# A dilated convolution in one list: more six-step groups, and every instruction placed one by one

## The chip, the cores and the metric

The kernel runs on one core of a Trainium2 chip. The metric is the device time of one execution in microseconds; the median of three runs of the kernel before is 263.8 us (262.93 to 263.85).

## The reference

The input `x` has 2 sequences of 16,000 time steps with 256 channels; `w` holds three taps of 256 by 512, `w_o` is 256 by 256, everything in bf16. It is a causal convolution of three taps with dilation 2, a gate, and a projection:

```
xp = jnp.pad(x, ((0, 0), (4, 0), (0, 0)))
h = sum over i of einsum('btc,cd->btd', xp[:, 4 - 2*i : 4 - 2*i + T, :], w[i])
z = tanh(h[..., :256]) * sigmoid(h[..., 256:])
return z @ w_o
```

## The kernel before

Time is cut into groups. A group of R rows (256, if nothing else is said) holds J steps per row, so it covers J times R time steps; its tile `xt` has channels on the partitions and one plane of R columns for each step. One group P (four steps, 160 rows) is computed directly. All others save multiplications: an output group is made from a few products of sums and differences of `xt`'s planes with sums of the weights, and is then put together by adding and subtracting the products.

- Kind B covers 4 steps with 4 products per block: operands `m`, `p`, `d0`, `d3`.
- Kind A covers 6 steps with 5 products: operands `u1`, `rm`, `rp`, `r0`, `ri`. The last four are each a sum of two tiles: `rp` is `f` plus `u1`, `rm` is `e` plus `u3`, `r0` is `u0` plus `uh`, `ri` is `u2` plus `ud`, where `u3`, `uh`, `ud` are `u1` times a constant. The second term is added onto the first, in place.

Each group has four blocks, one for each 128 of the 512 output channels. For a block the steps are, by the letters of the plan: F, M, L, Z (first, mid, last, zero) accumulate their products in PSUM bank `b`, I (inf) in bank `a`. Between them other engines read the bank: ScalarE copies it after F into `ss` (c, line 432); VectorE makes `hh` from `ss` and `b` (h), writes `a` from `ss` and `b` (a, on line 435 like the others), and for kind A `yy` from `hh` and `b` (y). Then ScalarE applies tanh or sigmoid to `b`, `a` and `yy` (line 475), VectorE multiplies the two (g, the gate, line 494), TensorE multiplies by `w_o` (P, line 512), and ScalarE or VectorE (v) converts the result (e, lines 537 and 521) for a store issued by SyncE.

Before, 13 groups are of kind A and 12 of kind B (10 of 256 rows, one of 160, one of 128), beside P. Four B groups come first, then A and B blocks alternate in proportion. The operands come from three places. VectorE makes most of them whole (128x1024, lines 380 and 382). GpSimd makes `ri` and many of B's in quarters (128x256, line 382), each held behind a VectorE instruction by a semaphore, so that it runs while VectorE works on PSUM. And the second terms of `rm`, `rp` and `r0` are added by an accumulating DMA from SBUF to SBUF, issued from GpSimd's queue (line 377):

```
        if name in BY_DMA:
            return nc.gpsimd.dma_start(out=G[name][:, :, :, :R], in_=b, accum_op=op)
```

The loads of `xt` are transposing DMAs on SyncE's queue (line 234), which also issues the stores. The order is written out by hand: `PLAN` has a line for each block's turn, with one column of letters for each engine. Loads are issued up to 15 turns ahead (`LOAD`).

Of the kernel before, what the change touches and what calls it, by code (L numbers as in the profile page):

```python
# [11 lines left out]

PLAN = """
 |  | m.0 d3.0 p.0 d0.0 G | 
F D D | c w |  | 
F L D | c d | a d3.1 G | wa.4 wa.3
F L Z I P P | c b e | a | wa.6
Z L F I | a b c | m.1 d0.1 p.1 a | wa.12'
F L Z I | a c b | m.2 g a | wa.5
L P F Z I | a e c b | d3.2 a | wa.2'  # L20
Z L F I | a b c | d0.2 u0.0 g a | wa.7
F L Z I | a c b | f.0 u1.0 a | wa.1
L F Z I | a c b | p.2 a u2.0 g | wa.14'
L Z F I P | a b e c | e.0 d3.3 a | wa.0
F P P Z L I | a c e e b | p.3 ud.0 g a | wa.11
L F I Z P P | a c b | u1.1 m.3 m.4 a | rp.0 ri.0'
F L Z P I P | a e e e b c | u3.0 e.1 uh.0 a d0.3 f.2 g | wa.10
F I Z L P | a c e b | u1.2 a | rm.0 ri.0'
L F Z I | a e c b | a g | r0.0
L Z I F P | a b c | u3.1 p.4 a | wa.8  # L30
Z L F P I | a b c e e | u0.1 uh.2 f.1 a d0.4 g | ri.0'
F I L P Z M P | c e a b | d3.4 u2.1 ud.1 a h | rp.1 rm.1 wa.15' wa.13' wa.9'
F Z L M I | a c e e b | g uh.1 a y h | d3.5' d3.5' ri.0'
P P Z F L I | y a b c | u3.2 e.2 a y | r0.1 ri.1 m.5
F L I Z M | a c y b | a u0.2 h | d0.5 d0.5
Z F L I M | a b c e | g a y h | r0.2 d0.5 ri.1
F P Z I L | a e c b y | g u2.2 a y | rm.2 ri.1 m.5' d0.5
F L P I Z M | a e c y b | a e.3 h | p.5
Z F I L M | a c b | g a y h | p.5 p.5 ri.1
P P F Z L I | a e e y c b | u0.3 a y | m.5 m.5'  # L40
L F I Z M | a c y b | ud.2 a u1.3 h | ri.2 ri.2'
Z P P F L I P M | a b e c e e | g u3.3 a y h | rp.2 p.5' p.6' d0.6'
F Z I L P | a e b c y | f.3 g a y | ri.2 d3.5
F L I Z M | a c y b | a u2.3 h | d3.5
Z F I L M P P | a c b e | g a y h | rp.3 rm.3 d0.6 ri.2
F Z I L P | a e e y b c | uh.3 e.4 ud.3 a y | d3.6 p.6 ri.3''
F L I Z M | a c y b | a u1.4 h | ri.3
Z F I L M P P P | a c b e | g a y h | m.6 d3.6
F Z P L I | a e y c b e e e | g u0.4 u3.4 f.4 a y | r0.3 ri.3 m.6''
F L P I Z M | a c y b | a ud.4 h | d0.6 d3.6 m.6  # L50
Z I F L | a b c | g a y | ri.3 m.6
F L P I Z M P | c a y b | u2.4 a h | ri.4' d3.6
F Z L I P M | a e e c b | e.5 uh.4 y a h | rp.4 p.6
F Z P L I | a y c b e e | g f.5 a y | rm.4 p.6' d0.6'
F P L Z M I | a c y b | g a h | r0.4 p.7 p.7 ri.4 d3.7 d3.7 m.7
F Z L P M I | a c e b e | u1.5 a y h | ri.4
I Z P L F P P | a e e b c y | u0.5 a y | ri.4
F L Z I M | a c b y | ud.5 u1.6 u2.5 a h u3.5 g | rp.5 ri.5''
F P Z L I P M | a c e e b | a y h | rm.5 d0.7 p.7
F Z I L P | a e y b c e | g uh.5 a y | m.7' ri.5  # L60
F L I Z P M | a c y b | g ud.6 a h | r0.5 ri.5' m.7'
F P Z L M I | a c b e e | e.6 uh.6 y a h | d3.7 d0.7
F P Z L I P | y e a b c | f.6 a y | m.7' ri.5
F L Z M I P | a c y b e | u0.6 g h u3.6 a | rp.6 p.7' d0.7' d0.7
F L P M Z I | a c e e e b | y a h | rm.6
Z I L F P | a y b c | u2.6 u1.7 a y g | m.8' m.8'
F P P L Z M I | a c e y b e e | g u3.7 a h | r0.6 ri.6' d3.7'
F Z L P I M | a c b | e.7 ud.7 a y h | p.8' ri.6' ri.6
F Z I L P P | a y b c | u0.7 u2.7 a y | p.8' ri.6'
F L P M Z I | a e c y e e b | uh.7 f.7 a h g | d0.8' ri.7'  # L70
Z I F L | a b c | u1.8 a y | rm.7 rp.7 m.8'
F P P L Z M I | a c e y b e | g a e.8 h | d3.8 ri.7
F Z I L M P | a c b e | g a y ud.8 h | p.8 d3.8 ri.7
F P Z I L P | a e c y b e | u3.8 f.8 a y | r0.7 d3.8' d0.8
L F I Z M P | a e c b y | a u0.8 h | d0.8 m.8
F Z P L P M I P | a c e e e b | e.9 g a y h | p.8 ri.7
Z F L I | a b c y | u1.9 g a y | rp.8 d3.8
F L I Z M P P | a c e b y | u2.8 ud.9 a h | rm.8 d0.8 d3.9'
Z F L P M P I P | a e c e e b | uh.8 g a y h | ri.8 ri.8
Z L F I | y a b e c | u3.9 u2.9 a y | r0.8 ri.8  # L80
F I Z L M P P | a c y b | f.9 u0.9 a h | ri.9' ri.8'
F L Z I M | a e e c b | g y a h | ri.9
F Z I L | y a b c e | f.10 g a y | rp.9 d0.9
F P P L Z M I | c a b y | u0.10 a h | rm.9 d0.9'
F Z I L P P M | a e c e b | e.10 g uh.9 y a h | r0.9 d3.9
F P Z L P I | a e e y b c e | m.9 u1.10 a y | ri.9' ri.9
F L I Z M P | c a e b y | p.9 a h | d0.9' d3.9' d3.9'
Z P F L I M | a b c e e | ud.10 g a y h | d0.9
F I Z P L P | a y b c | u2.10 g a y | rp.10 ri.10 d3.10 d0.10
F L I Z M | a c e y b | a u1.11 h |   # L90
Z P F L P I | a b c e | u3.10 g y uh.10 a | rm.10 ri.10'
F L P Z I M | a e c b e y | e.11 a u2.11 h | ri.10'
F I Z L P P M | c a e b | ud.11 f.11 a y u3.11 h | r0.10 ri.10'
F I Z L | a e c y b e | g uh.11 a y | d3.10 d0.10'
L P F P Z M I | a c b y | g a h | rm.11 d0.10 d3.10
F Z L I M P | a c e b | u1.12 a y h | ri.11' ri.11'
F Z I L | a e c b y | p.10 m.10 y a | rp.11 ri.11
L P F P Z M I | a c e b y e | a u3.12 u0.11 h f.12 g | d3.10
Z F P L I P M P | a c b e | a y h | r0.11 ri.11 d0.10
I F Z L P | a e y e b e c | g e.12 ud.12 y a | rm.12  # L100
F P P M Z L P I | c e a b y e | p.11 u2.12 uh.12 a h g | d3.11' ri.12'
F I L P Z M P | a c e b | y a h | d0.11 d3.11
F Z L P I | y e a b c e e | u0.12 m.11 a y | rp.12 r0.12 ri.12''
F P Z L M I | c a b y | a h g | 
F Z L P I M P | a c b e e e | a y h | d0.11 ri.12
F Z L P I | a c b e y | g a y | d3.11 ri.12
L F I Z M P | a c y b e e | a g h | 
Z F L P I P M | b c a | y a h | 
F P Z L I | a e e y b c e | y a | d0.11
F P L Z M I | c a b y | a h g | d0.11  # L110
F P L Z I P | a e c b e | a y | d3.11
F I Z L | a c y b | g a | 
L P I F Z P | a e b c e | a g | 
Z I F L P P | a c b E | a v | 
L Z I P p | a b | a g v | 
Z I P p P | a e b | v | 
H H | a e E | g v | 
R R |  |  | 
 | e | v | 
"""  # L120


@with_exitstack
def kernel(
    ctx: ExitStack,
    tc: tile.TileContext,
    x: bass.AP,
    w: bass.AP,
    w_o: bass.AP,
    out: bass.AP,  # L130
):
# [33 lines left out]
    for b in range(B):  # L165
        t = 0
        if b == 0:
            t = group("P", b, 0, 160)
# [374 lines left out]

# [182 lines left out]
```

## Time and profile before

| what | value |
|---|---|
| median of three runs | 263.8 us |
| profiled execution, span from first to last instruction | 261.4 us |
| taken as the profiled execution's own time (the span and 2.4 us around it, to the median) | 263.8 us |
| TensorE busy | 256.5 us, 98% |
| ScalarE busy | 243.7 us, 93% |
| VectorE busy | 240.5 us, 92% |
| GpSimd busy | 136.2 us, 52% |
| matmuls | 1484 |

A page of the profile gives the busy time of each engine (PE is TensorE, DVE is VectorE, ACT is ScalarE, POOL is GpSimd, SP is SyncE), the busy share in 40 slices, the DMA queues, the chain of work that ended last and the costliest groups of instructions. In a group's row stand the line, the engine, the operation, the tile written and those read, the shape, the count, then the busy time in us and the mean duration of one in ns, then the idle time before them. A duration includes an overlap with the next instruction, so that counts times means add up to more than the engine's busy time.

### The profile page before, as it was taken

To read this page: it belongs to the slowest core of one execution; us is meant where nothing else is said; L and a number is where in the kernel's file an instruction comes from. 1 tells how busy PE (TensorE), PEld (TensorE's weight loads), DVE (VectorE), ACT (ScalarE), POOL (GpSimd) and SP (SyncE) were. 2 spreads that over 40 slices of the span, in tenths; PEclk is the share of its full clock that TensorE was granted. 3 is DMA by queue.
4 is the path that set the end of the run, shared out by engine and by line. 5 is a ranking of instruction groups with operands and counts; after the bars stand their busy time and mean duration, and the time that the engine had idled before them with its cause. 6 is when DMAs were issued, how large, how long until landed. Compare 5 with 4: busy or idle time off the path is not lost.

```text
span 261.4 us, 4534 instructions
## 1 busy us (share of the span) xinstructions
PE 256.5 (98%) x1484; PEld 144.2 (55%) x1484; DVE 240.5 (92%) x401; ACT 243.7 (93%) x492; POOL 136.2 (52%) x204
## 2 busy tenths in 40 slices
PE   8999999999999999999999999999999999999993
PEld 5654565545545555555555555555555555665682
DVE  2899999999999999999999999999999999977773
ACT  4989998999999999999999999999999999999993
POOL 1033355687765577956757685643746453431100
PEclk9999999999999999999999999999999999999999
DMA  6999979999969667969895799959825574462115
GB/s 185 215 168 212 262 177 174 227 211 179 212 152 232 139 147 143 228 147 230 197 197 135 175 214 190 239 160 201 237 41 127 149 152 116 129 160 109 76 61 210
DMA packets 81663, 45.20 MB, mean 173 GB/s; under 512 B 68936, under 2 KB 70216, under 8 KB 81640
## 3 DMA queue, kind: packets, MB, share of 16 engines
q1 hardware_dynamic: 75112, 33.74, 54.6%
q0 software_dynamic: 5616, 10.23, 23.2%
q10 hardware_dynamic: 912, 0.95, 1.1%
q8 instruction: 11, 0.18, 0.3%
q14 instruction: 12, 0.10, 0.1%
HBM read 1.25 MB, written 16.38 MB: 67 GB/s over the span
## 4 chain that ended last, share of the span: by engine, by line
PE 97%; DMA 1%; DVE 0%; issue 0%
PE b L401 57%; PE o_ps L512 21%; PE a L401 16%; PE b L421 1%; PE a L421 1%; DMA xn<-in_x_dram 1%; PE tp L308 0%; DVE osb L521 0%; PE fill L248 0%
## 5 line engine op out<-in xcount | busy, mean ns | idle before, releaser
L435 DVE SCALAR_TENSOR_TENSOR a<-ss,b 128x512 f32<-128x512 f32 (+2 forms) x100 | 67.1, 672 | 7.9 <-ACT sg L475 3.1
L537 ACT CAST osb<-o_ps 128x512 bf16<-128x512 f32 x119 | 69.8, 622 | 0.8 <-PE o_ps L512 0.7
L512 PE MATMUL o_ps<-wo_sb,zz 128*128 128x256 bf16 x496 | 70.5, 273 | 0.0
L432 ACT COPY ss<-b 128x512 f32<-128x512 f32 (+2 forms) x100 | 59.6, 597 | 4.6 <-PE b L401 3.5
L512 PEld LDWEIGHTS <-zz 128*128 128x128 bf16 x496 | 48.4, 98 | 25.2 <-DVE zz L494 0.2
L401 PEld LDWEIGHTS <-w_sb 128*128 128x128 bf16 x400 | 39.0, 98 | 36.8 <-issue 0.2
L382 POOL TENSOR_TENSOR u<-u,ud 128x256 bf16<-128x256 bf16 x52 | 39.8, 772 | 24.9 <-DVE zz L494 9.1
L382 POOL TENSOR_TENSOR d<-xt 128x256 bf16<-128x256 bf16 (+2 forms) x56 | 33.4, 606 | 32.7 <-DVE zz L494 13.0
L494 DVE TENSOR_TENSOR zz<-th,sg 128x1536 bf16<-128x1536 bf16 (+2 forms) x52 | 40.9, 788 | 0.5 <-ACT sg L475 0.2
L435 DVE SCALAR_TENSOR_TENSOR yy<-hh,b 128x512 f32<-128x512 f32 x52 | 35.4, 680 | 1.9 <-PE b L401 1.8
L435 DVE SCALAR_TENSOR_TENSOR hh<-ss,b 128x512 f32<-128x512 f32 x52 | 35.4, 681 | 1.2 <-PE o_ps L512 0.5
L475 ACT ACTIVATE sg<-b 128x512 bf16<-128x512 f32 (+2 forms) x50 | 30.5, 610 | 2.1 <-PE b L401 1.4
L475 ACT ACTIVATE th<-b 128x512 bf16<-128x512 f32 (+2 forms) x50 | 30.5, 610 | 1.9 <-PE b L401 1.6
L475 ACT ACTIVATE sg<-a 128x512 bf16<-128x512 f32 (+2 forms) x50 | 31.0, 619 | 0.0
L401 PE MATMUL b<-f,wp_sb 128*128 128x512 bf16 x104 | 30.9, 379 | 0.0
L401 PE MATMUL b<-u,w_sb 128*128 128x512 bf16 x104 | 30.9, 379 | 0.0
L401 PE MATMUL a<-u,w_sb 128*128 128x512 bf16 x104 | 30.9, 379 | 0.0
L401 PE MATMUL b<-u,wa_sb 128*128 128x512 bf16 x104 | 30.9, 379 | 0.0
L401 PE MATMUL b<-e,wm_sb 128*128 128x512 bf16 x104 | 30.9, 378 | 0.0
L475 ACT ACTIVATE th<-a 128x512 bf16<-128x512 f32 (+2 forms) x50 | 30.5, 614 | 0.3 <-PE a L401 0.2
L401 PEld LDWEIGHTS <-wp_sb 128*128 128x128 bf16 x200 | 19.5, 98 | 20.1 <-issue 0.7
L401 PEld LDWEIGHTS <-wm_sb 128*128 128x128 bf16 x200 | 19.5, 98 | 17.0 <-issue 0.4
(59 smaller groups left out, 342.7 us busy)
## 6 DMA issues: line engine op xcount, KB each, us to landing
out_dram<-osb SPq DMA_DIRECT2D x26, 384.0 KB, 2.6
out_dram<-osb SPq DMA_DIRECT2D x23, 256.0 KB, 3.0
f<-u POOLq DMA_DIRECT2D x13, 256.0 KB, 3.5
e<-u POOLq DMA_DIRECT2D x13, 256.0 KB, 4.4
u<-uh POOLq DMA_DIRECT2D x13, 256.0 KB, 5.3
w_sb<-in_w_dram ACTq DMA_DIRECT2D x3, 256.0 KB, 4.1
xt<-in_x_dram SPq DMA_TRANSPOSE x25, 7.2
xn<-in_x_dram SPq DMA_DIRECT2D x1, 160.0 KB, 3.2
```

Of the source, the lines that this page charges most:

```text
L382: ins = eng.tensor_tensor(out=o, in0=a, in1=b, op=op)
L401: nc.tensor.matmul(G[bank, oi][:, :2 * R], lhsT=wmat[:, ct, osl], rhs=G[mv][:, :, ct, :R], start=which == "first" and ct == 0, stop=ct == ...
L421: nc.tensor.matmul(G[bank, oi][:, :4 * r].rearrange("p (j r) -> p j r", j=4), lhsT=w_taps[tap][:, ct, osl], rhs=xt[:, j0:j0 + 4, ct, c0 + ...
L432: nc.scalar.copy(out=G["ss", oi][:, :n], in_=G["b", oi][:, :n])
L435: return note(nc.vector.scalar_tensor_tensor(out=out, in0=in0, scalar=scalar, in1=in1, op0=ALU.mult, op1=op))
L475: nc.scalar.activation(out=G[name, dt][:, j:j + 2, :R], in_=G[bank, oi][:, :2 * R].rearrange("p (q r) -> p q r", q=2), func=(ACT.Tanh, ACT ...
L494: note(nc.vector.tensor_tensor(out=G["z"][:, dt, :, :n], in0=G["th", dt][:, :, :n], in1=G["sg", dt][:, :, :n], op=ALU.mult))
L512: nc.tensor.matmul(o_ps[:, q, :], lhsT=z, rhs=wo_sb[:, dt, :], start=dt == 0 and (q == 0 or len(dts) == NT), stop=dt == NT - 1, skip_group ...
L537: copy(out=osb[:, 2 * jp:2 * jp + 2, :], in_=o_ps[:])
```

## The change

The groups are written down (`GROUPS`): P, 18 groups of kind A, three B groups of 256 rows and one of 160. `ORDER` runs their blocks group after group: the three B groups, then all A groups, then the last B. The plan with a line per turn is replaced by one list of 1,745 tokens in which every instruction has its place among all engines' instructions. Besides:

- `ri` gets its second term by accumulating DMA too. In all 69 such DMAs are listed (token `rp.3d`), where there were 39; two `rm` and one `ri` are left to VectorE (`rm.5`, `rm.9`, `ri.8`).
- Quarters of `u0`, `u1`, `u2`, `e`, `f` and of the last B groups' operands are given to GpSimd one by one (`u0.3q38`). The number behind q says how many VectorE instructions back the one lies that the quarter waits for.
- For 31 of the 72 A blocks `hh` is a plain copy of the bank made by ScalarE (k), and `yy` is then made from that copy and `a` instead of from `hh` and `b`.
- VectorE makes 25 of the output conversions (v), instead of 5.
- Loads (x) and stores (s) are tokens of the list; the rotating buffers of operands, `hh`, th, sg and output tiles are fixed slots numbered by group or block; the scratch tiles of the weights lie in the A groups' gate tiles.

The diff, cut to its core:

```
-PLAN = """
- |  | m.0 d3.0 p.0 d0.0 G | 
-F D D | c w |  | 
...
+GROUPS = (
+    "P160 A A A A A A A A B B B",
+    "A A A A A A A A A A B160",
+)
+ORDER = """
+9 9 9 9 10 10 10 10 11 11 11 11 1 1 1 1 2 2 2 2 ... 21 21 21 21 22 22 22 22
+"""
+PLAN = """
+m.0 d0.0 d3.0 p.0 D D m.1 D F G d F c G F c p.1 L d3.1q1 c P A w L d0.1 x e0 L d3.1q1 Z A I b f.0 P a u1.0 Z d3.1q1
+F A b I c u0.0 F a Z x d0.2 c I g wa.3q1 b L L a A d3.1q12 P e1 F A wa.5q12 Z c ud.0 I u1.1 b Z a x u3.0 L m.2 b F
...
+P y f.13q158 Z Y e75 M ri.12d e.13 b Z ri.13d e76 h48 I b F rm.13d u1.14 P a g f.13q1 L c F y Y I y A P rp.13d c M
...
-    wu_sb = [[ss_pool.tile([P, D2], f32, name=f"wu{tap}", tag=tag) for tag in ("hh", "yy")] for tap in range(K)]
+    wu_ct = [z_pool.tile([P, K, D2], f32, name="wu", tag="zz6") for _ in range(CT)]
+    wu_sb = [[wu_ct[ct][:, tap, :] for ct in range(CT)] for tap in range(K)]
...
-    BY_DMA = ("rm", "rp", "r0")
...
-                G[name] = pool.tile([P, 2, CT, RG], bf16, name=name, tag=name)
-        if name in BY_DMA:
+                G[name] = slot(name, G["n"], [P, 2, CT, RG])
+        if eng is None:
             return nc.gpsimd.dma_start(out=G[name][:, :, :, :R], in_=b, accum_op=op)
...
+    def second(blk, on_act):
...
+        if on_act:
+            G["k", oi] = True
+            nc.scalar.copy(out=G["hh", oi][:, :n], in_=G["b", oi][:, :n])
+            return
         stt(G["hh", oi][:, :n], G["ss", oi][:, :n], 1.5, G["b", oi][:, :n], ALU.subtract)
...
-            stt(G["y", oi][:, :n], G["hh", oi][:, :n], 2.0, b)
+            if ("k", oi) in G:
+                stt(G["y", oi][:, :n], G["hh", oi][:, :n], -2.0, G["a", oi][:, :n])
+            else:
+                stt(G["y", oi][:, :n], G["hh", oi][:, :n], 2.0, b)
...
+    def on_gpsimd(token):
+        token, _, back = token.partition("q")
+        behind = made_v[-1 - int(back)]
...
+        had = quarters.get((g, name), 0)
+        quarters[g, name] = had + 1
+        pre(g, name, nc.gpsimd, slice(had, had + 1), behind=behind)
...
+    for token in PLAN.split():
+        what = token[0]
+        if "." in token:
+            if "q" in token:
+                on_gpsimd(token)
+            elif token[-1] == "d":
+                pre(*group_of(token[:-1]), None)
             else:
-                made.append(todo.pop(0))
...
+                note(pre(*group_of(token), nc.vector))
+        elif what in "FMLZI":
+            product(next(kinds[what]), {"F": "first", "M": "mid", "L": "last", "Z": "zero", "I": "inf"}[what])
...
+        elif what == "s":
+            store(*stores[int(token[1:])])
+        elif what == "x":
+            load(next(to_load))
```

More of the change, by code (lines that the diff above doesn't have):

```diff
@@ L209, with slot @@
     ctx.enter_context(tc.manual_schedule())
+    SLOTS = {"m": 2, "p": 2, "d0": 3, "d3": 3, "u0": 3, "u1": 3, "u2": 3, "e": 3, "f": 3, "u3": 2, "uh": 2, "ud": 2, "hh": 3, "th": 2, "osb": 3, "odd": 3}
+    def slot(name, n, shape, dtype=bf16, kind=None):
+        return ring_pool.tile(shape, dtype, name=name, tag=f"{name}.{n % SLOTS[kind or name]}")
     def warm_up(n):
@@ L351, in operand @@
         }[name]()
+    blocks = [0] + [g for g, oi in seq if oi == 3]
+    a_seq = [blk for blk in seq if blk[0] in As]
     def hold(ins, behind):
@@ L441, in halfway @@
         n = 2 * G["R"]
[L442 removed]
+        G["hh", oi] = slot("hh", a_seq.index(blk), [P, 2 * RG], f32)
+        if on_act:
+            G["k", oi] = True
+            nc.scalar.copy(out=G["hh", oi][:, :n], in_=G["b", oi][:, :n])
+            return
         stt(G["hh", oi][:, :n], G["ss", oi][:, :n], 1.5, G["b", oi][:, :n], ALU.subtract)
@@ L465, in activate @@
         if (name, dt) not in G:
-            G[name, dt] = act_pool.tile([P, J, RG], bf16, name=name, tag=f"{name}{J}")
+            same = [at for at in blocks if groups[at]["J"] == J]
+            G[name, dt] = slot(f"{name}{J}", NT * same.index(g) + dt, [P, J, RG], kind="th")
         if G["kind"] == "P":
@@ L705 @@
+    assert next(todo, None) is None and next(to_load, None) is None
 _INS = ['x', 'w', 'w_o']
```

386 lines of the change are left out of this document (126 added, 260 removed).

## The prediction

> **What bounds the kernel now.** I read the page first: the span, TensorE's row, the engines' shares of the chain that ended last, and the two large DMA queues.
>
> ```profile
> span 261.4 us, 4534 instructions
> PE 256.5 (98%) x1484; PEld 144.2 (55%) x1484; DVE 240.5 (92%) x401; ACT 243.7 (93%) x492; POOL 136.2 (52%) x204
> ...
> q1 hardware_dynamic: 75112, 33.74, 54.6%
> q0 software_dynamic: 5616, 10.23, 23.2%
> ...
> PE 97%; DMA 1%; DVE 0%; issue 0%
> ```
>
> The chain is TensorE nearly from end to end. Whether the others have room is a question by stage, so next come the windows: for each stretch its length, each engine's busy time with its instructions, the granted clock and the DMA engines' share.
>
> ```profile
> 0.00:10.00 10.00, 9.16 (x65) 5.82 (x66) 5.10 (x8) 6.44 (x14) 0.81 (x8) 1.00 0.79 196
> 10.00:20.00 10.00, 10.00 (x59) 5.41 (x58) 8.90 (x18) 8.54 (x18) 2.55 (x5) 1.00 1.12 183
> ...
> 240.00:250.00 10.00, 10.00 (x68) 6.48 (x67) 7.25 (x13) 9.98 (x24) 1.20 (x3) 1.00 0.21 81
> 250.00:262.00 12.00, 7.30 (x67) 6.20 (x64) 6.17 (x12) 7.22 (x19) 0.00 (x0) 0.95 0.39 147
> ```
>
> ```profile
> 20.00:60.00 40.00, 40.00 (x217) 21.00 (x215) 39.55 (x68) 37.51 (x74) 22.08 (x32) 1.00 1.10 207
> 60.00:200.00 140.00, 140.00 (x784) 76.26 (x782) 136.80 (x223) 134.86 (x268) 92.17 (x130) 1.00 0.83 181
> ```
>
> Between 10 and 250 us TensorE never stops. VectorE is busy 98.9% of 20 to 60 us and TensorE still does not wait: nearly full engines can be fed here. The DMA share over 1 means that several queues' packets were in flight on one engine. So the time can fall only by less TensorE work, and it falls by that much only if the others keep up.
>
> **TensorE.** The chain in order of time gives the price of a piece (start, length, what):
>
> ```profile
> 58.93 1.29 PE b L401 x6
> ```
>
> A matmul of 512 columns takes 1.29/6 = 0.215 us, one of 256 I take at half, 0.108. Products of 512 columns go from 840 (13 A groups x 4 blocks x 10 matmuls, 10 B groups x 4 x 8) to 816 (18 x 40 + 3 x 32); the 32 of 256 columns go with the 128-row group; those of 160-row groups and the projection stay. Saved: 24 x 0.215 + 32 x 0.108 = 8.6 us, all on the path. If nothing else bound, the span would be 261.4 - 8.6 = 252.8 us.
>
> **VectorE and ScalarE.** Groups by form (busy us, mean ns of one, idle before):
>
> ```profile
> L435 DVE SCALAR_TENSOR_TENSOR a<-ss,b 128x512 f32<-128x512 f32 x92 | 63.4, 690 | 3.9 <-PE b L401 2.6 <-ACT th L475 0.6
> L432 ACT COPY ss<-b 128x512 f32<-128x512 f32 x92 | 55.9, 608 | 4.6 <-PE b L401 3.5 <-DVE u L382 0.3 <-ACT sg L475 0.3
> ...
> L475 ACT ACTIVATE sg<-b 128x512 bf16<-128x512 f32 x46 | 28.6, 621 | 1.9 <-PE b L401 1.4
> L382 DVE TENSOR_TENSOR u<-xt 128x1024 bf16<-128x1024 bf16 x39 | 27.9, 720 | 0.0
> ...
> L494 DVE TENSOR_TENSOR zz<-th,sg 128x1536 bf16<-128x1536 bf16 x26 | 24.8, 954 | 0.5 <-ACT sg L475 0.2
> ...
> L475 ACT ACTIVATE th<-yy 128x512 bf16<-128x512 f32 x26 | 17.2, 660 | 0.2 <-DVE yy L435 0.2
> L494 DVE TENSOR_TENSOR zz<-th,sg 128x1024 bf16<-128x1024 bf16 x20 | 13.7, 683 | 0.0
> ...
> L380 DVE TENSOR_SCALAR ud<-u 128x1024 bf16<-128x1024 bf16 x13 | 5.7, 441 | 0.0
> ...
> L521 DVE CAST osb<-o_ps 128x512 bf16<-128x512 f32 x5 | 3.3, 685 | 0.6 <-PE o_ps L512 0.6
> ```
>
> The smaller forms I price at half of these; other B operands and two gate forms are priced by the rows shown. VectorE, counted in the two instruction lists: whole sums 87 to 64, -23 x 0.72 = -16.6; four small ones gone, -1.4; scalings 39 to 54, +15 x 0.441 = +6.6; PSUM sums of 512 columns 196 to 197, +0.7, and four small ones gone, -1.4; gates of 1536 columns 26 to 36, +9.5, of 1024 20 to 6, -9.6, small ones -0.7; conversions 5 to 24 and a small one, +13.3. Sum +0.4 us: nothing. ScalarE: `ss` copies 92 to 84 and four small, -6.1; 31 bank copies k, +18.8; tanh and sigmoid of `b` and `a` -16 x 0.621 and eight small, -12.4; of `yy` 52 to 72, +13.2; conversions 119 to 100 and a small one, -12.1. Sum +1.4 us.
>
> So both keep their work in a shorter span. VectorE did 14.0 us of its 240.5 in the first 20 us, whose work is nearly the same; the other 226.5 in 252.8 - 20 is 97%, below the 98.9% shown above. ScalarE: 243.7 + 1.4 - 15.0 = 230.1 in 232.8, 99%; the row of 240 to 250 shows it at 9.98 of 10. At 252.8 us both are full but not over; about 2 us more make room. The new wait, I behind `yy` in the 31 k blocks (`yy` reads `a` before I adds to it), has in the list at least one other TensorE token between, and what queues behind it is TensorE itself: I take it at nothing while VectorE is on time, and at what VectorE is late otherwise.
>
> **GpSimd.**
>
> ```profile
> L382 POOL TENSOR_TENSOR u<-u,ud 128x256 bf16<-128x256 bf16 x52 | 39.8, 772 | 24.9 <-DVE zz L494 9.1 <-DVE yy L435 4.4 <-DVE u L382 3.5
> ...
> L377 POOL DMA_DIRECT2D f<-u x13 | 11.9, 918 | 0.0
> ```
>
> Quarters of 256 columns go from 124 to 164 (40 x 0.772 = 31 us), DMA issues from 39 to 69 (30 x 0.918 = 28). 136.2 + 59 = 195 us of some 257: 76%, not a bound over the whole.
>
> **The DMA engines** are where the work goes. The 39 accumulating DMAs took 23.2% of 261.4 us = 60.6 us of all 16 engines, 1.55 us each; 30 more cost 46.6 us. Loads and stores move nearly the same bytes. From 77.8% (203.4 us) the two queues come to 250 us in about 255: full. What this costs depends on when an accumulating DMA lands against when its product is due. Before, by windows (median us from issue to landing, last), first 20 to 60 us, then 60 to 200:
>
> ```profile
> e<-u POOLq DMA_DIRECT2D x3, 256.0 KB, 7.7
> u<-uh POOLq DMA_DIRECT2D x3, 256.0 KB, 8.3
> f<-u POOLq DMA_DIRECT2D x2, 256.0 KB, 5.6
> ```
>
> ```profile
> f<-u POOLq DMA_DIRECT2D x9, 256.0 KB, 3.4
> e<-u POOLq DMA_DIRECT2D x8, 256.0 KB, 4.3
> u<-uh POOLq DMA_DIRECT2D x7, 256.0 KB, 5.3
> ```
>
> Means of the three: 7.2 us at a DMA share of 1.10, 4.3 at 0.83. By the Trainium skill, "DMA: Bandwidth & Descriptors", section "Anatomy of one DMA", a DMA from GpSimd's queue takes about 2.0 us plus its bytes at 436 GB/s, an estimate of 2.6 us for these 256 KB; by it none would be late and the sum would be 252.8 us. The trace does not agree: the best median is 3.4.
>
> The list tells how much TensorE work stands between a DMA's token and the first product that reads its result: with 0.43 us a token (two matmuls of 512 or four of 256 columns), the shortest lead of the 18 A groups, in order, is 13, 12, 14, 19, 14, 17, 12, 13, 16, 15, 16, 15, 11, 12, 16, 18, 16 and 12 tokens: 4.7 to 8.2 us. If every DMA took L, TensorE would lose in each group what L exceeds the shortest lead by. Summed: L = 4.3 loses nothing; 5.8 loses 3.9 us (1.1 at the lead of 11, 0.6 at each 12, 0.2 at each 13); 6.4 loses 8.8; 7.2 loses 18.7. Loads per us are as many as between 60 and 200 us before, but accumulating DMAs nearly twice as many (69 in some 205 us against 24 in 140), so L lies between 4.3 and 7.2; I take the middle, 5.8.
>
> **The start and the queues passed.** The first A group's load moves from fourth to third place on SyncE's queue, and its first product from the seventeenth block to the thirteenth. The first 20 us show TensorE busy for 19.16; a late load there would cost once, between nothing and some 2 us (the share of 1.12 says that the DMA engines are full); I take nothing, as the load itself comes earlier too. Stores stand in SyncE's queue ahead of loads as before; the shortest lead of a load is 7 us of TensorE tokens, most have 10 to 28, so a store that waits for its conversion costs nothing.
>
> **Sum.** 261.4 - 8.6 + 3.9 = 256.7 us of span. The profiled execution's own time is taken as the median of the runs, 263.8, so 2.4 us lie around the span: 259.1 us.
>
> **Rivals.**
>
> *All of it is kept.* The DMAs land within their leads, since tokens of loads are spread and at most few DMAs meet. For: 4.3 us in the calmer window. Against: full DMA engines. 252.8 + 2.4 = 255.2 us; with ScalarE or VectorE short of room, up to 257.
>
> *The DMA engines become the bound (slower).* Place: the first product after each accumulating DMA, in the middle 200 us. Price: as above, decided at L = 6.4 us; at 6.8 it loses some 13 us (268 us), at 7.2 18.7 (273.9 us). For: 7.2 was measured where the share was 1.10. Against: there eight loads were issued in 40 us.
>
> *VectorE held up by GpSimd (slower).* A row of the order in time of VectorE, then one of GpSimd's:
>
> ```profile
> 105.06 0.98 DVE L382 TENSOR_TENSOR u<-xt 128x1024 bf16<-128x1024 bf16 x1
> ```
>
> ```profile
> 104.19 1.29 POOL L382 TENSOR_TENSOR p<-xt 128x256 bf16<-128x256 bf16 x2 [0.39 <-DVE zz L494]
> ```
>
> The sum at 105.06 began while GpSimd's pair ran until 105.48 and took 0.98, where the mean of these sums is 0.72. Before, every quarter was held behind one of the last few VectorE instructions; after, 167 of 196 wait for one ten or more back, which by then is long done. VectorE has 168 instructions on SBUF alone; each tenth that meets a quarter costs 17 x 0.26 = 4.4 us. With the 6 us idle at the start and about 4 at the end VectorE needs 240.9 + 10, plus 1% = 253; it decides against the change from one in four on (+11 us, 264 + 2.4 = 266). The Trainium skill, "SBUF — State Buffer", section "SBUF: two separate sides", says that the port pair is an exclusive lock for a whole instruction, and the loser waits; the two rows agree. Against: 138 of those 167 stand in the list just ahead of a VectorE instruction on PSUM.
>
> *Nearly even.* L between 6.25 and 6.5 (7.3 to 9.8 us lost), or VectorE met by one in six: 262.5 to 265.1 us.
>
> **Chances.** A measurement of this kernel tells about 0.5% from no change, so the bounds are 262.5 and 265.1. Forecast (some loss, 256 to 262.5) 0.36; all kept 0.17; nearly even 0.14; DMA bound 0.23; VectorE held up 0.10. Faster 0.53, same 0.14, slower 0.33. The range goes from the full gain, 254.8, to L = 6.9 (some 14.3 us lost), 269.5; beyond it I leave about 0.15. The cases of a gain alone lie from 254.8 to 262.5.
>
> **What would show it.** Right: 1428 matmuls; TensorE's busy time near 248 with 4 us of new waits, put down to DMAs onto `f`, `e` or `u`; VectorE and ScalarE busy near 241 and 245; q0's packets at 69/39; landings with medians of 5 to 6.5 us. All kept: landings near 4.3 and no TensorE wait. DMA bound: medians over 6.4, GpSimd queues in step with them. VectorE held up: sums on SBUF with means well over 720 ns, and TensorE waiting for `a`, `yy` or `hh`. Wrong altogether: a TensorE clock under 1, or a busy time of VectorE or ScalarE off by over 5 us.

## The result, and the profile after

The changed kernel takes 290.86 us (median of three runs, 290.72 to 293.87) where the one before takes 263.8: 1.108 times as long, with an interval of 1.100 to 1.115. The forecast was 259.1 us and its range ended at 269.5. The profiled execution has a span of 288.9 us. From its page the span, the busy times, the two large DMA queues and the chain:

```profile
span 288.9 us, 4582 instructions
...
PE 256.9 (89%) x1428; PEld 139.1 (48%) x1428; DVE 270.0 (93%) x400; ACT 244.1 (84%) x487; POOL 194.1 (67%) x274
...
q1 hardware_dynamic: 74168, 33.71, 48.5%
q0 software_dynamic: 9936, 18.09, 36.7%
...
PE 51%; DVE 26%; issue 10%; SPq 4%; DMA 4%; ACT 3%; DVEq 0%; ACTq 0%
```

TensorE issues the 1428 matmuls that were counted, and ScalarE's 244.1 and GpSimd's 194.1 us are near the count, GpSimd's by luck: its DMA issues average 1.06 to 1.25 us by group and its quarters of `u` 0.87, more than the 0.92 and 0.77 that were counted with, but they overlap. VectorE's time is not as counted: 270.0 us for a list that the forecast priced at 240.9. The chain, 97% TensorE before, is now a quarter VectorE. The windows that were shown of before (20 to 60 us and 60 to 200 us), and two short ones in which most is lost:

```profile
20.00:60.00 40.00, 37.06 (x192) 18.50 (x191) 38.98 (x63) 34.98 (x70) 30.10 (x42) 1.00 1.07 195
60.00:200.00 140.00, 124.97 (x687) 67.01 (x686) 138.25 (x199) 123.68 (x246) 111.09 (x152) 0.99 0.93 200
```

```profile
100.00:120.00 20.00, 14.34 (x72) 7.29 (x71) 18.87 (x22) 12.79 (x26) 11.73 (x17) 0.91 0.59 118
200.00:220.00 20.00, 16.78 (x79) 8.45 (x79) 16.85 (x25) 13.51 (x27) 9.53 (x14) 0.83 0.70 137
```

From 60 to 200 us VectorE is 98.8% busy and TensorE 89%, where before they were at 98% and 100%. Between 100 and 120 us VectorE is busy for 18.87 us with only 22 instructions, 0.86 us each, where before it did 223 in 136.8 us, 0.61 each. The granted clock of TensorE falls to 0.91 and 0.83 in the stretches in which it waits longest. What TensorE waits for (us in total, times, longest):

```profile
PE b L337 <- DVE hh L371: 8.0, 5, 5.9
PE b L337 <- DVE a L371: 5.4, 6, 2.7
PE o_ps L456 <- DVE zz L438: 5.0, 3, 4.1
PE a L337 <- DVE yy L371: 2.8, 4, 1.0
PE a L337 <- DVE a L371: 2.1, 2, 1.9
```

All five are waits for VectorE; of the others none is over 1.3 us and none is for a DMA. VectorE's groups by form show which of its instructions grew, after and then two of before:

```profile
L318 DVE TENSOR_TENSOR u<-xt 128x1024 bf16<-128x1024 bf16 x35 | 38.6, 1108 | 0.9 <-DMA xt<-in_x_dram 0.9
L438 DVE TENSOR_TENSOR zz<-th,sg 128x1536 bf16<-128x1536 bf16 x36 | 36.7, 1023 | 0.0
L371 DVE SCALAR_TENSOR_TENSOR hh<-ss,b 128x512 f32<-128x512 f32 x41 | 27.7, 677 | 0.0
...
L316 DVE TENSOR_SCALAR uh<-u 128x1024 bf16<-128x1024 bf16 x18 | 18.2, 1009 | 0.0
```

```profile
L435 DVE SCALAR_TENSOR_TENSOR hh<-ss,b 128x512 f32<-128x512 f32 x52 | 35.4, 681 | 1.2 <-PE o_ps L512 0.5 <-PE a L401 0.2 <-PE b L401 0.2
...
L380 DVE TENSOR_SCALAR uh<-u 128x1024 bf16<-128x1024 bf16 x13 | 5.5, 420 | 0.0
```

The sums `u` take 1108 ns on average (720 before), the scalings `uh` 1009 (420 before), while instructions that read PSUM, such as `hh` with 677, are what they were (681). The means hide the shape of it: 25 of the 35 sums `u` take under 0.7 us, and the four longest 2.3 to 6.87. Two answers of the order in time, VectorE's and GpSimd's, at the longest one:

```profile
195.11 0.68 DVE L371 SCALAR_TENSOR_TENSOR a<-ss,b 128x512 f32<-128x512 f32 x1
195.71 6.87 DVE L318 TENSOR_TENSOR u<-xt 128x1024 bf16<-128x1024 bf16 x1
202.49 1.27 DVE L371 SCALAR_TENSOR_TENSOR hh<-ss,b 128x512 f32<-128x512 f32 x2
```

```profile
195.57 0.87 POOL L313 DMA_DIRECT2D f<-u  x1 [0.30 <-POOL f L318]
196.18 0.97 POOL L318 TENSOR_TENSOR e<-xt 128x256 bf16<-128x256 bf16 x1
196.81 1.58 POOL L318 TENSOR_TENSOR f<-xt 128x256 bf16<-128x256 bf16 x2
198.06 0.94 POOL L318 TENSOR_TENSOR u<-xt 128x256 bf16<-128x256 bf16 x1
...
201.09 0.92 POOL L318 TENSOR_TENSOR e<-xt 128x256 bf16<-128x256 bf16 x1
```

One VectorE sum of 0.72 us stands for 6.87 us, beside nine quarters. The GpSimd rows hold the clue: the quarters begin 0.6 us apart (196.18, 196.81 ... 198.06) but take 0.92 to 0.97 each, so each begins some 0.3 us before the one ahead has ended; and the run begins right behind a DMA issue. Counted over the records, 66 of the 153 quarters that follow a quarter begin over 0.1 us before its end, and 31 of the 41 that follow an issue; before it was 1 of 119 and 6 of 35. Every run of overlapping quarters in this trace, but for one of three quarters, starts with an issue.

### The profile page after: what moved, and what is told of

The parts are those of the page before. It is cut to its first block, busy times and chain, and to the rows that moved or that the text cites. A ratio compares the mean times of both kernels' runs of the same rounds, so it can differ in the third digit from the quotient of the medians.

```text
span 288.9 us, 4582 instructions
## 1 busy us (share of the span) xinstructions
PE 256.9 (89%) x1428; PEld 139.1 (48%) x1428; DVE 270.0 (93%) x400; ACT 244.1 (84%) x487; POOL 194.1 (67%) x274
## 3 DMA queue, kind: packets, MB, share of 16 engines
q0 software_dynamic: 9936, 18.09, 36.7%
HBM read 1.25 MB, written 16.38 MB: 61 GB/s over the span
## 4 chain that ended last, share of the span: by engine, by line
PE 51%; DVE 26%; issue 10%; SPq 4%; DMA 4%; ACT 3%; DVEq 0%; ACTq 0%
PE b L337 31%; PE o_ps L456 13%; PE a L337 7%; DVE a L371 7%; DVE yy L371 4%; SPq L168 4%; DVE zz L438 3%; DVE hh L371 3%; DVE u L318 3%; DMA xt<-in_x_dram 2%; DMA w_sb<-in_w_dram 1%; DVE ud L316 1%; DVE u L316 1%; DVE osb L465 1%; ACT th L419 1%
## 5 line engine op out<-in xcount | busy, mean ns | idle before, releaser
L318 POOL TENSOR_TENSOR u<-xt 128x256 bf16<-128x256 bf16 x76 | 61.9, 868 | 10.5 <-PE b L337 8.6
L371 DVE SCALAR_TENSOR_TENSOR a<-ss,b 128x512 f32<-128x512 f32 (+1 forms) x88 | 59.4, 677 | 5.4 <-PE b L337 5.0
L368 ACT COPY ss<-b 128x512 f32<-128x512 f32 (+1 forms) x88 | 52.4, 600 | 10.9 <-PE b L337 10.5
L318 POOL TENSOR_TENSOR f<-xt 128x256 bf16<-128x256 bf16 x52 | 44.8, 900 | 14.9 <-PE b L337 4.8
L337 PE MATMUL b<-f,wp_sb 128*128 128x512 bf16 x144 | 44.0, 389 | 8.4 <-DVE hh L371 8.0
L318 DVE TENSOR_TENSOR u<-xt 128x1024 bf16<-128x1024 bf16 x35 | 38.6, 1108 | 0.9 <-DMA xt<-in_x_dram 0.9
L419 ACT ACTIVATE sg<-b 128x512 bf16<-128x512 f32 (+1 forms) x44 | 27.0, 614 | 10.1 <-PE b L337 10.0
L318 POOL TENSOR_TENSOR e<-xt 128x256 bf16<-128x256 bf16 x32 | 31.0, 1019 | 5.4 <-DVE hh L371 3.0
L419 ACT ACTIVATE th<-b 128x512 bf16<-128x512 f32 (+1 forms) x44 | 27.1, 615 | 5.2 <-PE b L337 3.1
L337 PEld LDWEIGHTS <-wp_sb 128*128 128x128 bf16 x176 | 17.2, 99 | 25.9 <-issue 11.8
L419 ACT ACTIVATE sg<-a 128x512 bf16<-128x512 f32 (+1 forms) x44 | 27.3, 620 | 1.1 <-PE a L337 1.1
## 6 DMA issues: line engine op xcount, KB each, us to landing
f<-u POOLq DMA_DIRECT2D x18, 256.0 KB, 5.0
u<-uh POOLq DMA_DIRECT2D x18, 256.0 KB, 4.7
u<-ud POOLq DMA_DIRECT2D x17, 256.0 KB, 4.4
e<-u POOLq DMA_DIRECT2D x16, 256.0 KB, 4.2
out_dram<-osb SPq DMA_DIRECT2D x8, 256.0 KB, 3.3
w_sb<-in_w_dram ACTq DMA_DIRECT2D x3, 256.0 KB, 4.1
```

Of the source, the lines that this page charges most:

```text
L318: ins = eng.tensor_tensor(out=o, in0=a, in1=b, op=op)
L337: nc.tensor.matmul(G[bank, oi][:, :2 * R], lhsT=wmat[:, ct, osl], rhs=G[mv][:, :, ct, :R], start=which == "first" and ct == 0, stop=ct == ...
L368: nc.scalar.copy(out=G["ss", oi][:, :n], in_=G["b", oi][:, :n])
L371: return note(nc.vector.scalar_tensor_tensor(out=out, in0=in0, scalar=scalar, in1=in1, op0=ALU.mult, op1=op))
L419: nc.scalar.activation(out=G[name, dt][:, j:j + 2, :R], in_=G[bank, oi][:, :2 * R].rearrange("p (q r) -> p q r", q=2), func=(ACT.Tanh, ACT ...
```

## The experiments

They are told in the order of the argument. Theory A: VectorE's instructions on SBUF are kept out while GpSimd's quarters read SBUF. Theory B: the DMA engines bind, as the prediction had it. Theory C: the list is too tight for TensorE, however long VectorE's instructions take. Ratios are to the kernel before, run on the same chip, with a 95% interval.

**Whose time is it: GpSimd's reads, or the DMA engines?** Three kernels leave part of the work out of the changed kernel.

```
-            ins = eng.tensor_tensor(out=o, in0=a, in1=b, op=op)
+            ins = eng.memset(o, 0.0) if eng is nc.gpsimd else eng.tensor_tensor(out=o, in0=a, in1=b, op=op)
```

> The changed kernel with GpSimd's quarter sums replaced by memsets of the same quarters (it leaves those sums out; no SBUF is read for them). Theory A: with the reads gone VectorE is not held up: VectorE busy 238-246 us, time 255-263 us. Theory B: 286-294 us, as all DMAs stay. Theory C: over 280 us.

Measured: 261.25 us, ratio 0.995 (0.992 to 0.999). From its page and its windows:

```profile
PE 249.6 (96%) x1428; PEld 138.8 (54%) x1428; DVE 240.8 (93%) x400; ACT 241.3 (93%) x487; POOL 117.8 (46%) x274
```

```profile
20.00:40.00 20.00, 18.14 (x90) 8.61 (x89) 18.67 (x32) 16.49 (x33) 13.79 (x22) 1.00 1.10 198
...
200.00:220.00 20.00, 20.00 (x116) 11.20 (x115) 19.32 (x33) 20.00 (x41) 10.99 (x28) 1.00 1.11 226
```

VectorE is back at 240.8 us, TensorE never waits in the late stretch, and its clock is 1.00 there. So 29.2 us of VectorE's time (270.0 - 240.8) come from GpSimd's sums, and theory C is out: the same list runs in 261.25 us.

```
-            return nc.gpsimd.dma_start(out=G[name][:, :, :, :R], in_=b, accum_op=op)
+            return nc.gpsimd.dma_start(out=G[name][:, 0, 0, :64], in_=b[:, 0, 0, :64], accum_op=op)
```

> The changed kernel with each of the 69 accumulating DMAs adding 64 of the 1024 columns of a partition (it leaves the rest of the second terms out); issues, waits and order unchanged. Theory A: still 280-293 us, VectorE still busy 262-272. Theory B: 255-265 us, with q0's share down from 36.7% to under 6%. Theory C: 280-293 us.

Measured: 290.45 us, ratio 1.104 (1.100 to 1.107): one sixteenth of the accumulating DMAs' bytes, their queue down from 36.7% to 7.1% of the DMA engines, and nothing changes. Both edits together:

> The changed kernel with memsets in place of GpSimd's quarter sums and with additions of 64 of 1024 columns by the 69 DMAs (both leave work out). It prices the DMA engines once VectorE is free: against the 261.25 us of memsets alone, theory A with cheap DMAs says 259-262 us (nothing or the start of the kernel alone), theory B says at least 3.9 us less, 257 us or lower.

Measured: 260.33 us, ratio 0.988 (0.984 to 0.991). With VectorE free the accumulating DMAs' bytes cost 0.9 us by the medians and 2 by the ratios (0.995 and 0.988), not the 3.9 forecast. That the DMA engines caused the loss is refuted, with VectorE held up and without.

**Holding the quarters.** In the changed kernel each quarter waits behind a VectorE instruction that is mostly long done. Here all of them wait behind the one listed just before them:

```
-        behind = made_v[-1 - int(back)]
+        behind = made_v[-1]
```

> The changed kernel with one thing other: every quarter sum on GpSimd waits for the VectorE instruction listed just before it (as if each token ended in q0), so that it starts beside the next one, mostly one on PSUM. Order of every engine unchanged. Theory A (VectorE's instructions on SBUF are locked out while GpSimd's quarters run back to back): VectorE's busy time falls from 270 to 241-246 us, the sums u<-xt from a mean of 1108 ns to under 760, the time to 258-268 us. Theory B (the DMA engines are the bound): no change, 288-294 us. Theory C (the list is too tight for TensorE whatever VectorE's durations are): over 280 us.

Measured: 271.12 us, ratio 1.032 (1.028 to 1.036); VectorE 254.2 us. It regains 19.7 of 27 us, less than expected. The reverse, in the kernel before, frees its quarters:

```
-            behind = made_v[-1 - token.count("'")]
+            behind = made_v[max(0, len(made_v) - 40)]
```

> The kernel before with one thing other: each GpSimd quarter waits for the VectorE instruction 40 back instead of one of the last three, so it runs as soon as GpSimd is free. Theory A: VectorE's sums on SBUF get longer (u<-xt from 720 ns to over 850), its busy time goes from 240.5 to 250 us or more, the time from 263.8 to 270-290 us. Theories B and C: 262-266 us.

Measured: 315.27 us, ratio 1.199 (1.196 to 1.203), more than expected: the holds alone were worth 51 us to the kernel before. Its longest instruction and the GpSimd rows beside it again show a gate of 0.95 us that stands for 7.82 us, beside a run that starts with an issue:

```profile
177.11 7.82 DVE L494 TENSOR_TENSOR zz<-th,sg 128x1536 bf16<-128x1536 bf16 x1
```

```profile
176.29 0.86 POOL L377 DMA_DIRECT2D f<-u  x1 [0.82 <-DVE f L382]
176.85 1.00 POOL L382 TENSOR_TENSOR m<-xt 128x256 bf16<-128x256 bf16 x1
177.49 0.93 POOL L382 TENSOR_TENSOR d<-xt 128x256 bf16<-128x256 bf16 x1
```

**A test that backfired.** A function rewrote the list so that each quarter stands just ahead of a VectorE instruction on PSUM, at most one per VectorE instruction and at most six late:

```
-    for token in PLAN.split():
+    for token in beside_psum(PLAN.split()):
```

> The changed kernel with GpSimd's quarters moved down the list, in GpSimd's order, each to just ahead of a VectorE instruction on PSUM and held behind the VectorE instruction before that; at most one quarter for each VectorE instruction, none right behind a DMA issue, and none later than six VectorE instructions or its reader. TensorE, VectorE, ScalarE and SyncE keep their order. Theory A (VectorE's instructions on SBUF wait for GpSimd's sums): holding alone left VectorE busy 254.2 us and the time at 271.1; with the quarters beside PSUM work VectorE falls to 242-248 us and the time to 260-266. Theory B (DMA engines): no gain over the 271.1 of holding alone, as the additions are issued later still: 271-278 us. Theory C (the list is too tight for TensorE): 268-272 us.

Measured: 318.84 us, ratio 1.213 (1.204 to 1.222). What TensorE's matmuls wait for:

```profile
PE b L337 <- DMA f<-u: 13.9, 4, 5.4
PE b L337 <- DMA e<-u: 7.6, 4, 4.1
PE a L337 <- DMA u<-ud: 7.2, 3, 5.9
```

The operands' second terms now come late: GpSimd is 61% busy and waits for VectorE, and the additions are queued behind its quarters. VectorE is at 257.4 us, not the 242 to 248 expected. The edit changed two things at once, and tells only that GpSimd cannot be spread out this far.

**How few holds are enough?** The trace of after names the nine VectorE instructions on SBUF inside whose record two or more quarters began. One quarter for each is held behind it:

```
+    HELD = {13: 34, 19: 45, 50: 107, 65: 136, 72: 147, 97: 188, 136: 275, 169: 330, 182: 348}
+    on_g = iter(range(1000))
...
-        behind = made_v[-1 - int(back)]
+        behind = made_v[HELD.get(next(on_g), len(made_v) - 1 - int(back))]
```

> The changed kernel with nine of its 196 GpSimd quarters held back, each behind one VectorE instruction: those nine VectorE instructions on SBUF inside whose record two or more quarters began (among them the scale by -0.5 that took 4.53 us and the sum that took 6.87 us). Nothing else differs. Their nine records add up to 27.7 us where the undisturbed means of the same forms add up to 5.8. Theory A in its sharp form (a VectorE instruction on SBUF is kept out until a whole back-to-back run of quarters is over, so a few long runs carry the loss): VectorE busy falls from 270 to 248-252 and the time to 268-276 us. Theory A as the prediction priced it (each meeting costs a part of one quarter): nine meetings at 0.3 to 0.4 us are 3 us at most, 287-290 us. Theory that the runs of quarters are only a symptom and move on to the next VectorE instruction: 284-293 us with VectorE still near 268.

> As the nine holds, but for every VectorE instruction on SBUF inside whose record a quarter began: the first such quarter, 56 in all, waits until that instruction has ended; the other 140 keep their places. Theory A, sharp: the nine hold nearly all, so 47 further holds bring VectorE to 243-248 and the time to 262-270 us, at most 8 us under the nine. If each meeting costs its own part, this one gains much more than the nine (over 12 us under them). If holding GpSimd back starves TensorE of its operands, as in the run with quarters beside PSUM instructions alone (318.8 us): over 280 us, with TensorE waiting for DMA additions.

Measured: nine holds 268.56 us, ratio 1.018 (1.014 to 1.023), VectorE 251.7 us; 56 holds 268.03 us, 1.017 (1.015 to 1.020), VectorE 251.3 us where 243 to 248 were expected. Nine of 196 quarters regain 22.3 of the 27 us, and 47 more add nothing. The nine records held 21.9 us too much, so the loss was where the trace showed it: in a few long instructions, not in many small meetings.

**One instruction alone.** Three kernels measure a single VectorE sum beside GpSimd sums, without the rest of the computation.

> Not the reference's computation: a kernel that measures one VectorE instruction alone, three times each, beside 0, 1, 2, 4 or 8 GpSimd sums of 128x256 bf16 issued back to back (or 8 memsets of that size). A short VectorE instruction on PSUM goes ahead, so that the first GpSimd sum is under way when the measured instruction begins. Forms: sum of 128x1024 bf16 on SBUF, scale of 128x1024 bf16, product of 128x1536 bf16, and a PSUM instruction of 128x512 f32. Theory A, sharp: the sum takes 0.7 us with none, 0.9-1.2 with one, and grows by 0.6-0.8 us with each further one, to 5-6.5 us with eight; scale and product grow by the same; PSUM form 0.68 us throughout; memsets cost nothing. If VectorE gets its turn after the quarter that is under way: 0.9-1.3 us with one and no more than 1.5 us with eight.

Its groups by form (mean ns of three):

```profile
L63 DVE TENSOR_TENSOR sum_one<-sa,sb 128x1024 bf16<-128x1024 bf16 x3 | 2.8, 947 | 0.0
...
L63 DVE TENSOR_TENSOR sum_eight<-sa,sb 128x1024 bf16<-128x1024 bf16 x3 | 2.8, 922 | 0.0
...
L63 DVE TENSOR_TENSOR sum_none<-sa,sb 128x1024 bf16<-128x1024 bf16 x3 | 2.1, 684 | 0.0
L63 DVE TENSOR_TENSOR sum_sets<-sa,sb 128x1024 bf16<-128x1024 bf16 x3 | 2.1, 684 | 0.0
```

The sharp theory fell: beside eight sums back to back VectorE waited for one, 0.24 us, as beside one. This is the price that the prediction had used (0.26). So a long run alone is not enough, and the kernel's runs must differ from these. Theory A2: the quarters overlap because they follow a DMA issue, and then the port pair of the prediction, which the two engines share, never comes free.

> Not the reference's computation: the VectorE sum of 128x1024 bf16 on SBUF alone again, twice each, now with GpSimd issuing an accumulating DMA (256 KB, SBUF to SBUF) right ahead of its sums of 128x256. In the run without issues each such VectorE sum took 0.92-0.95 us beside 1, 2, 4 or 8 sums that ran in step, 0.07 us apart, against 0.68 alone; in the changed kernel the instructions that took 4.53 and 6.87 us stood beside sums that had followed a DMA issue and whose records overlap, the next beginning 0.3 to 0.8 us before the one ahead has ended. Theory A2 (behind a DMA issue GpSimd's sums overlap, so the port is never free until the last has ended): with one issue ahead VectorE's sum takes 1-1.7 us with one GpSimd sum, grows by 0.6 us with each further one, to 4.5-6 us with eight, likewise with two issues ahead; with eight in step, and with eight that wait behind ScalarE until the issue is over, 0.9-1.0 us. Theory that it is the operands' form or other traffic in the kernel and not the issue: 0.9-1.3 us in every case.

Measured: 1.06 us behind an issue with two, four and eight sums alike, 1.05 with one, 0.68 with two issues and eight. A miss again. But the sums of these two kernels all wrote one tile, and stood 0.07 us apart even behind the issue. With an output for each:

```
+    gs = [tile_of(f"gq{n}", 256) for n in range(8)]
...
-                g = nc.gpsimd.tensor_tensor(out=g3[:], in0=g1[:], in1=g2[:], op=ALU.add)
+                g = nc.gpsimd.tensor_tensor(out=gs[k][:], in0=g1[:], in1=g2[:], op=ALU.add)
```

> Not the reference's computation: the VectorE sum of 128x1024 bf16 alone once more, with every GpSimd sum of a run writing a tile of its own (in the two runs before, all wrote the same tile, and stood 0.07 us apart, with and without an issue ahead; VectorE got in after one of them, 0.92 to 1.06 us). 1, 2, 4 or 8 sums in step, 1, 2, 4 or 8 right behind the issue of an accumulating DMA, and 8 that wait until the issue is over. If only an overlap behind an issue keeps VectorE out to the end: in step 0.7-1.1 us whatever the number, behind the issue 1-1.3 us with one and 0.55 to 0.65 more with each further one (4-6 us with eight), 0.7-1.1 us with eight that wait. If every run without gaps does: in step with eight 4-6 us too, and with the eight that wait. If neither: all under 1.3 us, and what differs in the kernel stays open.

```profile
L96 DVE TENSOR_TENSOR sum_iss_eight<-sa,sb 128x1024 bf16<-128x1024 bf16 x2 | 10.8, 5380 | 0.0
...
L96 DVE TENSOR_TENSOR sum_iss_four<-sa,sb 128x1024 bf16<-128x1024 bf16 x2 | 5.8, 2914 | 0.0
L96 DVE TENSOR_TENSOR sum_iss_two<-sa,sb 128x1024 bf16<-128x1024 bf16 x2 | 3.4, 1679 | 0.0
L96 DVE TENSOR_TENSOR sum_iss_one<-sa,sb 128x1024 bf16<-128x1024 bf16 x2 | 2.3, 1148 | 0.0
L96 DVE TENSOR_TENSOR sum_gap_eight<-sa,sb 128x1024 bf16<-128x1024 bf16 x2 | 1.5, 731 | 0.0
...
L96 DVE TENSOR_TENSOR sum_step_eight<-sa,sb 128x1024 bf16<-128x1024 bf16 x2 | 1.4, 683 | 0.0
```

Behind an issue VectorE's sum takes 1.15, 1.68, 2.91 and 5.38 us with one, two, four and eight sums: 0.6 us for each further one, to the end of the run. Eight in step (each begins as the one before ends) cost it nothing, and eight that wait until the issue is over 0.05 us (0.73). There the wait falls on GpSimd: its second sum takes 1.10 to 1.15 us, the others 0.66. So, for an instruction alone, the cause of the long ones is settled: sums that overlap behind the issue of an accumulating DMA. Issues of other DMAs were not tried.

**The same in the kernel.** The 41 quarters that come right behind an issue are held behind the VectorE instruction listed just before them, and in a second kernel the 155 others instead:

```
+    added = []
...
-        behind = made_v[-1 - int(back)]
+        behind = made_v[-1 if added else -1 - int(back)]
+        added.clear()
...
+                added.append(token)
```

> The changed kernel with all quarters that come right behind a DMA issue on GpSimd's list (41 of 196) held behind the VectorE instruction listed just before them; the other 155 keep their holds. Theory A2 (the runs behind an issue carry the loss, and a wait there lets the issue end first): most of what holding all 196 regained (19.7 us), 268-276 us. Theory A without A2 (any quarter held helps alike): 41 of 196 regain about a fifth, 284-289 us.

> The complement: the 155 quarters that do not come right behind a DMA issue are held behind the VectorE instruction listed just before them, the 41 behind an issue keep their holds. A2: a quarter that waits further down a run still breaks it, but the run's first quarters stay overlapped; 276-289 us, clearly above the kernel that holds the 41. A without A2: four fifths of the 19.7 us, 272-278 us, below the kernel that holds the 41.

Measured: the 41 take 266.08 us, ratio 1.010 (1.008 to 1.012), the 155 others 274.61 us, 1.042 (1.040 to 1.044). A fifth of the quarters regains 24.8 us, the other four fifths 16.3. The 41 do even better than all 196 (271.12). Both kernels are faster than theory A2 expected (268 to 276 and 276 to 289), and the 155 lie in the range of its rival (272 to 278). But the rival had the 41 at 284 to 289 us, behind the 155; the order is A2's. Last, a kernel that takes away the overlap and holds nothing more against VectorE, by letting each quarter wait for the quarter before it:

```
+            on_g.append(hold(hold(weights_a(2 * K + int(token[3:])), behind), on_g[-1]))
...
-        pre(g, name, nc.gpsimd, slice(had, had + 1), behind=behind)
+        on_g.append(hold(pre(g, name, nc.gpsimd, slice(had, had + 1), behind=behind), on_g[-1]))
```

> The changed kernel, with every GpSimd sum waiting for the GpSimd sum before it to have ended; no hold against VectorE is changed, the order neither. Sums that overlap behind an issue then fall into step from the second on, at the price of about 0.12 us for each sum that follows at once (0.745 against 0.62 us from start to start in the runs alone), at most 23 us of GpSimd's idle 95. Theory A2 (the overlap is what keeps VectorE out): VectorE's longest instructions fall from 6.87 and 4.53 us to under 2, its busy time from 270 to 246-253, 262-269 us. Theory that it is the meetings as such, and holding GpSimd back behind VectorE is what helped: 280-293 us.

Measured: 273.7 us, ratio 1.039 (1.037 to 1.041). From its page:

```profile
PE 253.8 (93%) x1428; PEld 138.0 (51%) x1428; DVE 256.0 (94%) x400; ACT 244.2 (90%) x487; POOL 205.5 (75%) x274
```

No quarter overlaps the one ahead of it any more (0 of 153), no VectorE instruction on SBUF takes over 2.2 us, and 17.2 of the 27 us are regained; the rival's 280 to 293 is out, though the expected 262 to 269 is not reached. VectorE is still at 256.0 us, 15 over the undisturbed 240.8: what is left are mostly single meetings (three instructions with two quarters each hold 3.3 of the 15 us), and GpSimd is 11 us busier (205.5).

**Looking for a version that beats both.** Three kernels build on the 41 holds: nine further holds at places that its profile still showed too long; the same for 21 places, with 14 quarters moved down the list by one to three VectorE instructions; and the nine with each quarter waiting for the one before.

> The kernel with 41 holds behind issues (266.1 us) with nine further quarters held, each behind a VectorE instruction on SBUF that its profile still shows at least 0.25 us too long. Those nine hold about 4 of the 10 us that VectorE still spends over its undisturbed durations. Theory A2: 262-266 us. Theory that holding more only moves the loss: 265-269 us.

> As the kernel with nine further holds, but for all instructions too long by over 0.2 us (21 of 24), and where the quarter stands ahead of the VectorE instruction in the list, it and the GpSimd steps between are moved to just behind it (14 places, by one to three VectorE instructions). Nothing else in the list changes. Theory A2: VectorE near 243, 259-264 us, below the kernel before if it is at the low end. Theory that holding back starves TensorE: 266-275 us, with TensorE waiting for DMA additions.

> The same in the kernel with the 41 holds behind issues and nine more (265.4 us). A2: what is left there of overlapping sums goes too, VectorE 244-247, 261-265 us. If GpSimd's extra 0.12 us a sum is by then on TensorE's path: 265-270 us, with TensorE waiting for DMA additions.

Measured: 265.44 us, ratio 1.008 (1.006 to 1.009); 271.24 us, 1.030 (1.028 to 1.031); 277.53 us, 1.052 (1.050 to 1.054). None falls below the kernel before. In the second, expected at 259 to 264 us, new long instructions appear elsewhere (a sum `u` of 3.55 us), and moving quarters costs more than it mends. The third is 12 us slower than the first, outside both of its ranges. Its chain shows part of the reason:

```profile
PE 31%; DVE 24%; DMA 15%; POOL 12%; issue 7%; ACT 5%; SPq 5%; DVEq 0%; POOLq 0%; ACTq 0%
```

GpSimd, which is not on the first kernel's chain, has 12% here, and DMAs 15% (5% there): runs of quarters, one by one, and then the additions behind them. TensorE waits 3.7 us for additions, where in the first it waits for none. VectorE is at 258.3 us (248.0 in the first), with more single meetings. How the 12 us divide between the two was not separated.

## Why the prediction was wrong

The step that failed is VectorE's term of +0.4 us: the sum took VectorE undisturbed, and the rival that would have filled the term, "VectorE held up by GpSimd", had a chance of 0.10. VectorE was busy 29.2 us longer. Both the rival's price and its count were too low.

- **The price.** The rival priced a meeting at 0.26 us, from one row in which a sum waited for the end of a single pair. A quarter in step costs that at most: 0.24 to 0.26 us alone, or nothing, with the wait on GpSimd's side. Behind an accumulating DMA's issue the price is the rest of the run, 0.62 us for each quarter in it. In after 57 VectorE instructions had a quarter begin inside them (over 0.05 us before their end); at 0.26 that is 15 us of VectorE, it was 29.2, and nine of the 57 carry 21.9.
- **The count.** The prediction set against the rival that 138 of 167 loosely held quarters stand in the list just ahead of a VectorE instruction on PSUM. Place in the list is not time: 81 of 196 quarters began inside one of those 57 VectorE instructions on SBUF. By the prediction's own rule, from one in four of 168 on, 57 alone decided against the change, even at 0.26 us each.
- **VectorE at +0.4 us.** The count was right, 240.8 us without meetings against 240.9, and so was the warning that VectorE has no room. The term was taken undisturbed although the change did two things at once: 30 more DMA issues on GpSimd's queue, and quarters right behind them whose holds are long over. Before, holds stood between, and 1 of 119 quarters overlapped.
- **The cover that the 97% forgot.** VectorE needed 97% of the shorter span, so nearly all of 29 us more had to go onto the path: 261.25 us without the meetings, 290.86 with them. The prediction's own path rule, VectorE's time plus 10 us plus 1%, gives 283 us of span for 270.0, of the 288.9: this step held nearly, only its input was wrong. The clock, which the prediction named as a sign of being wrong altogether, fell with TensorE's waits, to 0.83 and 0.91 for a while; TensorE's busy time is 256.9 us against 249.6.
- **TensorE, -8.6 us.** Nearly right: 249.6 us in the kernel without the sums' reads, against 247.9 by the sum. That this kernel's 261.25 us stands only 2 us over the forecast is luck in part. Without meetings and with small additions the sum's span is 252.8 us, and 258.7 was measured: 5.9 us more, 1.9 of it in TensorE's busy time (249.8) and the rest in its waits, half of that between 20 and 40 us. The additions' term, 2 to 3 us too dear, hid part of it. And 1.8 us lie around the span (290.72 against 288.9), not 2.4.
- **The DMA engines, +3.9 us.** The packets' time was right (36.7% of 288.9 us over 69 is 1.54 us each). In after, with its slower pace, the additions' medians are 4.2 to 5.0 us; in the kernel without the sums' reads, which keeps the forecast's pace, they are near the 5.8 that was taken:

```profile
f<-u POOLq DMA_DIRECT2D x18, 256.0 KB, 5.5
u<-uh POOLq DMA_DIRECT2D x18, 256.0 KB, 6.1
u<-ud POOLq DMA_DIRECT2D x17, 256.0 KB, 6.0
e<-u POOLq DMA_DIRECT2D x16, 256.0 KB, 4.8
```

  But there they cost 0.9 to 2 us and not 3.9: the step from landings to losses, which let every DMA meet its group's shortest lead at one and the same L, was too dear. The rival that the prediction thought likeliest on the slow side (0.23) did not occur.
- **The start, nothing.** Wrong by about the bound given, 2 us: the kernel without the sums' reads loses 1.86 us of TensorE between 20 and 40 us (18.14 of 20.00), behind late loads.

## What to carry to other kernels

Before quarters, halves or other small work are given to GpSimd, look in the order in time at what stands ahead of them: behind an accumulating DMA that GpSimd itself issues, its next sums can overlap (31 of 41 did) and can keep a VectorE instruction on SBUF waiting to the end of the run. Not every one waits: between 186 and 195 us of after, with issues inside the run, seven took their usual time. A wait right behind the issue (41 holds) regained 25 of 27 us; holding all 196 regained 20, and spreading them out lost 28 more. And a mean in a group's row that rises by half can be nine instructions out of hundreds: sort them by length before pricing a mechanism by its typical case.

## What the runs showed of the hardware

- GpSimd's sums behind an accumulating DMA's issue overlap: 0.62 us from start to start, with records of 0.92 to 0.97 us. In step they also start 0.62 us apart, with records of 0.66: the issue makes the records longer, not the pace slower. The trace of the single instruction shows it:

```profile
61.34 0.87 POOL L80 DMA_DIRECT2D acc<-src  x1 [2.24 <-ACT mark L78]
61.95 5.29 POOL L87 TENSOR_TENSOR gq<-ga,gb 128x256 bf16<-128x256 bf16 x8
```

  The first sum begins 0.26 us before the issue has ended. The Trainium skill, "GPSIMD Engine Reference", section "2.1 Instruction dispatch", says that consecutive instructions of this engine are no barrier between its eight cores, each of which goes on when its own share is done, and section "4. When to use GPSIMD" that a pair of the cores writes a DMA's descriptors. By these the pair would be behind the other six from the issue on, and some core would read SBUF at every moment. The longer records at an unchanged pace fit that, but no run here shows single cores.
- A wait for its own previous sum brings GpSimd back into step (sums 0.07 us apart in the two kernels with one output tile, 0 of 153 overlapping in the kernel that waits one by one). So can a data dependence that is there by accident, which hid the effect in two experiments.
- The rule that the prediction quotes from the Trainium skill, "SBUF — State Buffer", section "SBUF: two separate sides", that the loser waits for a whole instruction, held for sums in step (0.24 us on VectorE, or 0.44 to 0.49 on GpSimd). Behind an issue the wait could be for the rest of the run: VectorE's instruction took up to 5.38 us alone (0.68 undisturbed) and 7.82 us in a kernel (0.95).
- GpSimd's memsets cost a VectorE sum nothing (684 ns with eight, as with none) and a gate nothing (951 ns), but a scaling alone took 645 ns beside eight and 419 beside none. In the kernel with memsets VectorE is at 240.8 us, the count without meetings (240.9).
